# Linear attention, then a gated MLP, on one core: features a step later, outputs held back into the next batch, copies in turns

## The chip, the cores and the metric

The kernel runs on one core of a Trainium2 chip. The metric is the time of the device in microseconds, from the launch's first to its last instruction; the median of several runs counts. The profile is one such execution, whose span (309.5 us) is a little shorter than the time that the runs give.

## The reference

There are 8 batches of 576 tokens. Phase A is attention with 8 heads of 64 channels and random features; phase B is a gated MLP that mixes tokens. Cut to what matters:

```
def phi(x):                                       # x: q or k, 64 channels -> 256 features
    proj = x @ w_phi                              # 128 wide
    proj = proj - max(abs(proj), axis=-1)
    return concat([exp(proj), exp(-proj)])
kv  = einsum('bhsf,bhsd->bhfd', phi(k), v);  z = sum(phi(k), axis=2)
x   = (phi(q) @ kv) / (phi(q) @ z + 1e-6)         # heads side by side: 512 channels

h = relu(x @ w_in);  u, v = h[..., :512], h[..., 512:]
v = (v - mean(v)) / sqrt(var(v) + 1e-6)
v = einsum('ts,bsd->btd', w_spatial, v) + b_spatial
out = (u * v) @ w_out
```

## The kernel before

**Tiles.** Each batch has four main blocks of 128 tokens and a tail of 64. Phase A works in units: a pair unit is two heads of one batch's main tokens, four for each batch; a tail unit is the tails of two batches (a group) for all heads. There are 32 pair units and 4 tail units, numbered in the order in which they run: a group's tail unit, then the four pair units of its even batch, then the four of its odd batch (in the first group one pair unit runs ahead of the tail unit). The program is fully unrolled, and a loop over steps writes out one unit per step, with the stages of earlier units beside it, as a software pipeline.

**One step** (`step`, L589). In step i these pieces are written, in this order, where u is the unit with number i minus a lag (L573):

- `p_features` (L257): `pf`, the projection of q by feature, minus its maximum. Eight small matmuls bring the maximum in from `mT`, two large ones add q's projection. Two PSUM banks. Lag 2.
- `p_keys`, `p_queries` (L266, L269): `pk` and `pq`, the projections by token. Two banks each. Lag 0.
- `e_features` (L272): four exponentials on ScalarE (ACT) turn `pf` into `qf`. Lag 2.
- `r_keys`, `e_keys` (L280, L289): the maximum of `pk` on VectorE (DVE), four exponentials into `kf` on ACT. Lag 0.
- `r_queries` (L294): the maximum of `pq` on DVE, kept in two bf16 parts in `mhl`.
- `a_scale` (L305): `em` on ACT, and v scaled by it into `vs` on GpSimd (POOL).
- `a_num` (L360): the numerators `pn` from `qf` and `kv`, and their division into `x` on DVE. Lag 3.
- `a_max_t` (L332): `mhl` transposed on PE and copied by DVE into `mT` (L335). Lag 1. There are three `mhl` and three `mT`, used in turns.
- `a_kv` (L337): `kv` of two heads on PE, copied out by ACT. Lag 2.
- `a_transpose` (L224) of the next unit, where no DMA has transposed it.
- `a_x_t` (L371): x transposed into `xT`, mostly by DMA. Lag 4. After the last pair unit of a batch, that batch's phase B is pushed into a queue (L631).

From step 8 on (`STRICT`) PE's instructions stay in the order in which they are written; the other engines' order is made by the framework's scheduler.

**Phase B** is a list of tasks for each batch (`b_tasks`, L548): a product for the tail's v, four products for v (`b_v`; ReLU into `vr` on ACT, statistics on DVE), the normalisation on POOL (`b_ln`: a root, L426 to L429, and four times `vn`, L433), four products for u (`b_u`, ReLU on ACT), four products with the spatial weights (`b_s`, each of five matmuls, and the gate on DVE, L493), four output products (`b_o`; `o_mm`, L510, copies the bank into `ob`, and a DMA writes it out), with the tail's tasks between. A task other than `b_s` is four matmuls of 512 columns. Each task takes one PSUM bank, held until the reading engine is through.

**The pace.** `fill` (L577) is called four times in a step. It adds credit, `RATE` = 3.75 us of PE work per step, and starts tasks while the credit covers half of the next one. What is left in the queue after the last step is run at the end (L671 to L673), where the outputs are copied by ACT (`drain`) and elsewhere by DVE (L515).

**PSUM.** All tiles come from one pool of eight banks under one tag (L57).

Of the kernel before, what the change touches and what calls it, by code (L numbers as in the profile page):

```python
# [16 lines left out]
def kernel(  # L17
# [15 lines left out]
    nc = tc.nc  # L33
# [8 lines left out]
    NP = H // 2  # L42
    NB = 4
# [22 lines left out]
    def matmul(**kw):  # L66
        on_pe(nc.tensor.matmul, **kw)

    def transpose(**kw):
        on_pe(nc.tensor.transpose, **kw)  # L70


    def pin(start):
        return lambda *a, **kw: tc.keep_in_program_order(start(*a, **kw))
# [123 lines left out]
    def transpose_spatial(i):  # L198

        pt = psum.tile([P, S], BF16, tag="bank", name="pt")  # L200
        if i < NB:
            sc = POS[i]
            for tp, c in enumerate(POS):
                transpose(out=pt[:, tp * P:(tp + 1) * P], in_=wsp[:, c, bass.ds(sc, P, step=NB)],
                                    identity=ident)
            transpose(out=pt[:, T0:S], in_=wspt[:, bass.ds(sc, P, step=NB)],
                                identity=ident[:TL, :TL])
            nc.vector.tensor_copy(out=w_spT[:, i, :], in_=pt)
            return
        for bl in range(2):  # L210
            lo = bl * TL
            for tp, c in enumerate(POS):
                transpose(out=pt[lo:lo + TL, tp * P:(tp + 1) * P], in_=wspr[:, c, :], identity=ident)
            transpose(out=pt[lo:lo + TL, T0:S], in_=wspt[:, T0:S], identity=ident[:TL, :TL])
            nc.vector.tensor_copy(out=w_spT[lo:lo + TL, NB + bl, :], in_=pt[lo:lo + TL, :])
        for bl, row in ((0, TL), (1, 0)):
            r = slice(row, row + 1)
            pin(nc.scalar.copy)(
                out=w_spT[r, NB + bl, 0:T0].rearrange("o (a b p) -> o a b p", a=2, b=2),
                in_=bsp_row[r, 0:T0].rearrange("o (p b a) -> o a b p", a=2, b=2))  # L220
            pin(nc.scalar.copy)(out=w_spT[r, NB + bl, T0:S], in_=bsp_row[r, T0:S])
# [67 lines left out]
    def e_keys(u, par):  # L289
        for s, sc in ((0, 1.0), (1, -1.0)):  # L290
            nc.scalar.activation(out=u["kf"][:, s, 4 * par:4 * par + 4, :], in_=u["pk"][par], func=AF.Exp,  # L291
                                 bias=0.0, scale=sc)
# [154 lines left out]
    def b_ln(b):  # L447
        d = st[b]
        rstd = root(d["mv"], slice(0, P), NB)
        for j in range(NB):  # L450
            normalize(d["vn"][:, j, :], d["vr"][j], rstd[:, j, :])

    def b_v_tail(g, bls):
        d = gs[g]
        r = slice(bls[0] * TL, (bls[-1] + 1) * TL)
        vr = s2.tile([P, HALF], BF16, tag="vr", name="vr", bufs=5)
        stats = small.tile([P, 6], FP32, tag="stats", name="stats")
        mv = small.tile([P, 1, 2], FP32, tag="mv_t", name="mv_t")
        v_mm(lambda kc: d["xTt"][:, kc, r], vr, r, stats, mv[:, 0, :])
        rstd = root(mv, r, 1)  # L460
        for bl in bls:
            r = slice(bl * TL, (bl + 1) * TL)
            normalize(vnt[g % 2][r, bl, :], vr[r], rstd[r, 0, :])

    def b_u(b, dc):
        d = st[b]
        pu = psum.tile([P, T0], FP32, tag="bank", name="pu")
        for kc in range(KC):
            matmul(out=pu, lhsT=w_in_bf[:, kc, dc * P:(dc + 1) * P], rhs=d["xT"][:, kc, :],
                             start=(kc == 0), stop=(kc == KC - 1))  # L470
        nc.scalar.activation(out=d["uT"][:, dc, :], in_=pu, func=AF.Relu, bias=0.0, scale=1.0)
# [38 lines left out]
    def o_mm(lhs, r):  # L510
        po = psum.tile([P, DM], FP32, tag="bank", name="po")
        for dc in range(KC):
            matmul(out=po[r], lhsT=lhs(dc), rhs=w_out_bf[:, dc, :], start=(dc == 0), stop=(dc == KC - 1))
        ob = s2.tile([P, DM], FP32, tag="ob", name="ob", bufs=5)
        (nc.scalar.copy if drain[0] else nc.vector.tensor_copy)(out=ob[r], in_=po[r])  # L515
        return ob

    def b_o(b, j):
        ob = o_mm(lambda dc: st[b]["uT"][:, dc, j * P:(j + 1) * P], slice(0, P))
        dst = bass.AP(tensor=out.tensor, offset=out.offset + b * S * DM + POS[j] * DM, ap=[[NB * DM, P], [1, DM]])  # L520
        nc.sync.dma_start(out=dst, in_=ob)

    def b_o_tail(g, bls):
        r = slice(bls[0] * TL, (bls[-1] + 1) * TL)
        ob = o_mm(lambda dc: gs[g]["uTt"][:, dc, r], r)
        for bl in bls:
            nc.sync.dma_start(out=out[2 * g + bl, T0:S, :], in_=ob[bl * TL:(bl + 1) * TL, :])


    units = []  # L530
# [8 lines left out]
    NU = len(units)  # L539
# [3 lines left out]
        return units[i] if 0 <= i < NU else None  # L543

    queue = []
    drain = [False]

    def b_tasks(b):  # L548

        g, bl = b // 2, b % 2  # L550
        mm = KC * T0 / 2400.0
        ms = (KC + 1) * T0 / 2400.0
        ts = [(mm, lambda: b_v_tail(g, [bl]))]
        ts += [(mm, lambda j=j: b_v(b, j)) for j in range(NB)]
        ts.append((0.0, lambda: b_ln(b)))
        if b == 0:
            ts += [(0.3, lambda i=i: transpose_spatial(i)) for i in range(NB + 1)]
        ts += [(mm, lambda dc=dc: b_u(b, dc)) for dc in range(KC)]
        tail = g in SPLIT or bl == 1
        bls = [bl] if g in SPLIT else [0, 1]  # L560
        if tail:
            ts.append((mm * len(bls) / 2, lambda: b_u_tail(g, bls)))
        ts += [(ms, lambda dc=dc: b_s(b, dc)) for dc in range(KC)]
        if tail:
            ts.append((ms * len(bls) / 2, lambda: b_s_tail(g, bls)))
        ts += [(mm, lambda j=j: b_o(b, j)) for j in range(NB)]
        if tail:
            ts.insert(len(ts) - 2, (mm, lambda: b_o_tail(g, bls)))
        return ts

    RATE = 3.75
    CAP = 2.5
    LAGS = dict(next=-1, maxima=1, features=2, sums=2, attention=3, out=4)  # L573
    FIRST = dict(next=-1, maxima=1, features=2, sums=2, attention=3, out=3)
    credit = [0.0]

    def fill(share):  # L577
        credit[0] = min(credit[0] + RATE * share, CAP)
        while queue and credit[0] >= queue[0][0] / 2:
            cost, task = queue.pop(0)  # L580
            task()
            credit[0] -= cost

    FT = dict(next=-1, maxima=1, features=2)

    def lag(u, what):
        return (FT if u["i"] == 1 else FIRST if u["pair"] and u["b"] == 0 else LAGS).get(what, 0)

    def step(i):  # L589

        if i == 0:
            a_transpose(units[0])

        def at_work(what):
            return [u for u in units[max(0, i - 5):i + 2] if u["i"] + lag(u, what) == i
                    and (u["pair"] or what not in ("sums", "attention", "out"))]

        def run(what, *fs):
            for u in at_work(what):
                for f in fs:  # L600
                    f(u)

        strict[0] = i >= STRICT
        if strict[0]:
            run("features", p_features)
        run("keys", p_keys)
        run("queries", p_queries)
        if strict[0]:
            run("features", e_features)
        run("keys", r_keys, lambda u: e_keys(u, 0))  # L610
        fill(0.25)
        run("queries", r_queries)
        run("keys", lambda u: e_keys(u, 1), a_scale)
        fill(0.25)
        for u in at_work("attention"):
            a_num(u)
            if u["pj"] == NP - 1:
                finish_batch(u, tail_num)
        fill(0.25)
        if strict[0]:  # L620
            run("maxima", a_max_t)
        run("sums", a_kv)
        run("next", a_transpose)
        if not strict[0]:
            run("features", p_features, e_features)
        fill(0.25)
        for u in at_work("out"):
            a_x_t(u)
            if u["pj"] == NP - 1:
                finish_batch(u, tail_x_t)  # L630
                queue.extend(b_tasks(u["b"]))  # L631
        if not strict[0]:
            run("maxima", a_max_t)
# [21 lines left out]
    for u in units:  # L655
# [4 lines left out]
        if u["pair"] and u["pj"] == 0 and u["b"] > 1:  # L660
# [3 lines left out]
            if u["b"] >= XB:  # L664
                for n, (x, part) in enumerate((("k", 0), ("q", 0), ("k", 1), ("q", 1))):
                    at(u["i"] - XP - 1 + n, cross, u["b"], x, part)
    for i in range(NU + 4):
        step(i)
        for f in io.get(i, []):
            f()  # L670
    drain[0] = True  # L671
    while queue:
        queue.pop(0)[1]()  # L673


# [28 lines left out]
```

## Time and profile before

The median of three runs is 311.28 us (310.86 to 311.39). From the page of the profile:

| | |
|---|---|
| span | 309.5 us, 8463 instructions |
| mean granted clock of TensorE | 0.982 |
| `qf` exponentials (L277, ACT) | 144, 74.4 us busy |
| `kf` exponentials (L291, ACT) | 144, 78.1 us busy |
| maxima of `pk` and `pq` (L286, L298, DVE) | 72 each, 46.4 and 49.9 us busy |
| copies of `ob` (L515) | 32 on DVE, 5 on ACT; full tiles 684 ns on DVE, 587 ns on ACT |
| steps 8 to 35, from `pk` to `pk` | 48.9 us to 259.8 us |

Busy time of an engine is counted with overlapping records joined. A wait is the idle time of an engine ahead of an instruction, put down to what that instruction was waiting for. PE is the stream of matmuls, PEld that of the weight loads, which lie beside it. The windows of the trace give, for a stretch of time, each engine's busy time and number of instructions, the TensorE clock that the throttle granted, and the traffic of the DMA engines. "L62" is the helper through which all matmuls are recorded, so matmuls are told apart by the tiles that they write.

### The profile page before, as it was taken

The page shows a single profiled execution, that of the slowest core. Times are in us where ns is not written, and L with a number is a line of the kernel's source. Part 1 is how long each engine was busy: PE and PEld are TensorE (multiplying, and loading weights), DVE is VectorE, ACT ScalarE, POOL GpSimd, SP SyncE. Part 2 cuts the span into 40 slices and gives each one's busy share as a digit, 9 for nine tenths or more (in the row PEclk, how much of TensorE's full clock was granted, in tenths as well). Part 3 has the DMA queues.
Part 4 walks back from the last instruction along what each step waited for, and adds up shares of the span by engine and source line. Part 5 has one row for each costly group of instructions (what it writes and reads, how often), then busy time and mean ns, then how long its engine had stood idle before and what let it go on. Part 6 is the DMA issues. An engine that isn't in the chain of part 4 may idle for free.

```text
span 309.5 us, 8463 instructions
## 1 busy us (share of the span) xinstructions
PE 255.8 (83%) x3251; PEld 157.4 (51%) x3294; DVE 231.6 (75%) x625; ACT 215.1 (69%) x487; POOL 174.4 (56%) x270
## 2 busy tenths in 40 slices
PE   3279789898997988878887999869797998998983
PEld 1157565666553565444454666435455664553441
DVE  6288997968987799955978799747977796666440
ACT  7558999797597767975487858875587768711603
POOL 8269892885238873497138962497139622620710
PEclk9999999999997999997999999997999999999999
DMA  7979999718652599788942599689912133004005
GB/s 184 233 115 194 205 252 153 168 63 101 153 141 51 84 210 227 147 183 111 155 153 51 154 192 196 161 188 116 207 73 53 17 83 124 4 0 138 0 2 169
DMA packets 82092, 40.35 MB, mean 130 GB/s; under 512 B 50626, under 2 KB 77442, under 8 KB 82052
## 3 DMA queue, kind: packets, MB, share of 16 engines
q1 hardware_dynamic: 54564, 28.33, 40.5%
q0 software_dynamic: 27328, 11.41, 33.5%
q8 instruction: 26, 0.43, 0.6%
q14 instruction: 14, 0.11, 0.1%
q10 hardware_dynamic: 160, 0.07, 0.1%
HBM read 32.85 MB, written 9.44 MB: 137 GB/s over the span
## 4 chain that ended last, share of the span: by engine, by line
PE 28%; DVE 26%; ACT 25%; POOL 8%; issue 7%; DMA 3%; POOLq 0%; DVEq 0%; ACTq 0%; another core or an unknown queue 0%
ACT qf L277 13%; ACT kf L291 9%; PE ps L62 8%; DVE stats L419 7%; PE pf L62 7%; DMA q_tl<-in_q_dram 3%; DVE x L358 3%; POOL vn L433 3%; DVE pq L298 3%; PE pu L62 3%; PE po L62 3%; PE pv L62 3%; DVE mk L286 3%; DVE ob L515 2%; DVE uT L493 2%
## 5 line engine op out<-in xcount | busy, mean ns | idle before, releaser
L277 ACT ACTIVATE qf<-pf 128x512 bf16<-128x512 f32 x144 | 74.4, 606 | 47.6 <-PE pf L62 47.6
L313 POOL TENSOR_TENSOR vs<-v_f,em 128x512 bf16<-128x512 f32 x64 | 65.4, 1041 | 61.9 <-ACT em L308 60.8
L291 ACT ACTIVATE kf<-pk 128x512 bf16<-128x512 f32 x144 | 78.1, 645 | 5.7 <-DVE mk L286 5.7
L286 DVE TENSOR_REDUCE mk<-pk 128x4 f32<-128x512 f32 x72 | 46.4, 686 | 15.1 <-PE pk L62 14.7
L298 DVE TENSOR_REDUCE pq<-pq 128x4 f32<-128x512 f32 x72 | 49.9, 693 | 1.5
L62 PE MATMUL ps<-w_spT,vn 128*128 128x64 bf16 (+1 forms) x244 | 40.6, 288 | 7.8 <-POOL vn L433 6.2
L493 DVE TENSOR_TENSOR uT<-ps,uT 128x512 bf16<-128x512 f32 x32 | 22.0, 687 | 23.8 <-PE ps L62 23.7
L419 DVE BATCH_NORM_STATS2 stats<-vr 128x6 f32<-128x512 bf16 (+1 forms) x40 | 26.9, 680 | 9.2 <-ACT vr L418 9.0
L62 PE MATMUL pu<-xT,w_in_bf 128*128 128x512 bf16 x115 | 32.0, 394 | 2.2 <-ACT kf L291 1.5
L418 ACT ACTIVATE vr<-pv 128x512 bf16<-128x512 f32 (+1 forms) x40 | 22.7, 613 | 14.8 <-PE pv L62 14.3
L62 PE MATMUL po<-w_out_bf,uT 128*128 128x512 bf16 x120 | 30.1, 380 | 1.9 <-ACT kf L291 0.9
L62 PEld LDWEIGHTS <-qf 128*128 128x128 bf16 (+1 forms) x640 | 25.9, 101 | 9.7 <-issue 1.5
L62 PE MATMUL pv<-w_in_bf,xT 128*128 128x512 bf16 x120 | 29.4, 379 | 0.6 <-issue 0.2
L62 PE MATMUL pn<-kv,qf 128*128 128x66 bf16 (+1 forms) x640 | 27.8, 196 | 1.8 <-ACT kf L291 0.8
L62 PE MATMUL pf<-mT,sel 64*128 64x128 bf16 x288 | 16.1, 225 | 14.8 <-DVE mT L335 13.5
L62 PEld LDWEIGHTS <-vn 128*128 128x128 bf16 x256 | 16.6, 99 | 22.1 <-POOL vn L433 9.9
L426 POOL TENSOR_SCALAR var<-mv_t 64x1 f32<-64x1 f32 x8 | 1.9, 239 | 44.3 <-DVE mv_t L420 30.7
L358 DVE TENSOR_TENSOR x<-pn,rc 128x256 bf16<-128x256 f32 x64 | 26.6, 420 | 0.4
L62 PEld LDWEIGHTS <-kf 128*128 128x128 bf16 x640 | 23.3, 99 | 7.0 <-ACT kf L291 2.0
L62 PE MATMUL pv<-vs,kf 128*128 128x66 bf16 x512 | 25.0, 195 | 0.8 <-ACT kf L291 0.8
L433 POOL TENSOR_SCALAR vn<-vr,rs 128x512 bf16<-128x512 bf16 x32 | 24.2, 769 | 0.8
L62 PEld LDWEIGHTS <-w_in_bf 128*128 128x128 bf16 x208 | 15.4, 99 | 14.2 <-issue 3.4
(103 smaller groups left out, 466.5 us busy)
## 6 DMA issues: line engine op xcount, KB each, us to landing
v_f<-in_v_dram SPq DMA_DIRECT2D x8, 1024.0 KB, 7.1
out_dram<-ob SPq DMA_DIRECT2D x32, 256.0 KB, 2.7
k_bf<-in_k_dram POOLq DMA_DIRECT2D x7, 512.0 KB, 6.5
q_bf<-in_q_dram POOLq DMA_DIRECT2D x7, 512.0 KB, 7.7
v_tl<-in_v_dram SPq DMA_DIRECT2D x8, 128.0 KB, 5.1
w_in_bf<-in_moe_w_in_dram POOLq DMA_DIRECT2D x2, 512.0 KB, 8.3
out_dram<-ob SPq DMA_DIRECT2D x8, 128.0 KB, 2.4
k_tl<-in_k_dram POOLq DMA_DIRECT2D x8, 64.0 KB, 7.0
```

The source lines that it names most:

```text
L62: r = f(*a, **kw)
L277: nc.scalar.activation(out=qf[:, s, 4 * par:4 * par + 4, :], in_=u["pf"][par], func=AF.Exp, bias=0.0, scale=sc)
L286: nc.vector.tensor_reduce(out=mk[:, par, :], in_=u["pk"][par], axis=AX.X, op=ALU.max, apply_absolute_value=True)
L291: nc.scalar.activation(out=u["kf"][:, s, 4 * par:4 * par + 4, :], in_=u["pk"][par], func=AF.Exp, bias=0.0, scale=sc)
L298: nc.vector.tensor_reduce(out=mq[:, 4 * par:4 * par + 4], in_=pq[par], axis=AX.X, op=ALU.max, apply_absolute_value=True)
L313: nc.gpsimd.tensor_tensor(out=vs[:, s, :, 0:D], in0=st[u["b"]]["v"][:, pj * H:(pj + 1) * H, :], in1=em[:, s, :].unsqueeze(2).to_broadcast( ...
L358: nc.vector.tensor_tensor(out=x, in0=pn[r, :, 0:D], in1=rc[r].to_broadcast([n, 4, D]), op=ALU.mult)
L418: nc.scalar.activation(out=dst[r], in_=pv[r], func=AF.Relu, bias=0.0, scale=1.0)
L419: nc.vector.bn_stats(out=stats[r], in_=dst[r])
L433: nc.gpsimd.tensor_scalar(out=dst, in0=src, scalar1=rs[:, 0:1], scalar2=rs[:, 1:2], op0=ALU.mult, op1=ALU.add)
L493: nc.vector.tensor_tensor(out=d["uT"][:, dc, :], in0=ps, in1=d["uT"][:, dc, :], op=ALU.mult)
L515: (nc.scalar.copy if drain[0] else nc.vector.tensor_copy)(out=ob[r], in_=po[r])
```

## The change

It does four things, from batch 2 (the second group) on, and the last two everywhere:

- The features of a unit are written one step later (lag 3 in place of 2), and with them the numerators (4 in place of 3) and x (5 in place of 4). The maxima are then a whole step old when `pf` wants them. The loop runs one step longer.
- The output tasks of a batch no longer end its own list. They are kept in `late` and put into the next batch's list, behind the normalisation and ahead of u, so that PE has more work while POOL normalises. The first two batches keep theirs; those of the last batch run at the very end.
- The copies of the outputs go to ACT and DVE in turns, all through.
- The pace is no longer fixed: at the start of each step it is the cost of what is in the queue, divided by the number of steps until the next batch is pushed, at most 4.0.

```diff
-        (nc.scalar.copy if drain[0] else nc.vector.tensor_copy)(out=ob[r], in_=po[r])
+        copies[0] += 1
+        (nc.scalar.copy if copies[0] % 2 else nc.vector.tensor_copy)(out=ob[r], in_=po[r])
...
         if b == 0:
             ts += [(0.3, lambda i=i: transpose_spatial(i)) for i in range(NB + 1)]
+        ts += late[:]
+        late.clear()
         ts += [(mm, lambda dc=dc: b_u(b, dc)) for dc in range(KC)]
...
-        ts += [(mm, lambda j=j: b_o(b, j)) for j in range(NB)]
+        late.extend((mm, lambda j=j: b_o(b, j)) for j in range(NB))
         if tail:
-            ts.insert(len(ts) - 2, (mm, lambda: b_o_tail(g, bls)))
+            late.insert(2, (mm, lambda: b_o_tail(g, bls)))
+        if b < 2:
+            ts += late[:]
+            late.clear()
         return ts
 
-    RATE = 3.75
+    RATE = [0.0]
+    MOST = 4.0
     CAP = 2.5
-    LAGS = dict(next=-1, maxima=1, features=2, sums=2, attention=3, out=4)
+    LAGS = dict(next=-1, maxima=1, features=3, sums=2, attention=4, out=5)
+    SECOND = dict(next=-1, maxima=1, features=2, sums=2, attention=3, out=4)
...
-        credit[0] = min(credit[0] + RATE * share, CAP)
+        credit[0] = min(credit[0] + RATE[0] * share, CAP)
...
-        return (FT if u["i"] == 1 else FIRST if u["pair"] and u["b"] == 0 else LAGS).get(what, 0)
+        return (FT if u["i"] == 1 else LAGS if u["g"] > 0 else FIRST if u["b"] == 0 else SECOND).get(what, 0)
+
+    pushes = [u["i"] + lag(u, "out") for u in units if u["pair"] and u["pj"] == NP - 1]
...
+        left = [p - i + 1 for p in pushes if p >= i]
+        RATE[0] = min(MOST, sum(c for c, _ in queue) / left[0]) if left else MOST
...
-    for i in range(NU + 4):
+    for i in range(NU + 5):
         step(i)
         for f in io.get(i, []):
             f()
-    drain[0] = True
-    while queue:
-        queue.pop(0)[1]()
+    for _, task in queue + late:
+        task()
```

More of the change, by code (lines that the diff above doesn't have):

```diff
@@ L545 @@
     queue = []
-    drain = [False]
+    late = []
+    copies = [0]
     def b_tasks(b):
```

## The prediction

> **What bounds the kernel now.** I read the page's busy row first, then the waits, then the span cut at the starts of steps (the first `pf` of a step on PE), then PE and DVE side by side in two stalls. The busy row:
>
> ```profile
> PE 255.8 (83%) x3251; PEld 157.4 (51%) x3294; DVE 231.6 (75%) x625; ACT 215.1 (69%) x487; POOL 174.4 (56%) x270
> ```
>
> PE looks nearly full, but that is too high: a lone 512-column matmul shows 0.39 us, while eight in a row (pu, at 132.65) take 1.90, so one more costs (1.90 - 0.39)/7 = 0.216 us. I therefore counted PE work from the order of its instructions at columns / 2.4 GHz, half of that for the paired 64-row matmuls (a `pk` group of 8 then starts 0.22 us before the next group, as the trace has it). The stages, in windows of the trace (columns: length, then busy time and count for PE, weight loads, DVE, ACT, POOL; granted clock; DMA):
>
> ```profile
> 48.90:86.60 37.70, 33.76 (x461) 21.76 (x465) 32.84 (x87) 29.97 (x70) 20.27 (x31) 1.00 0.68 127
> 86.60:123.30 36.70, 32.63 (x453) 20.28 (x457) 30.36 (x83) 28.24 (x66) 22.62 (x35) 0.95 1.02 141
> 123.30:191.80 68.50, 58.65 (x775) 36.06 (x787) 54.14 (x144) 50.33 (x118) 42.23 (x66) 0.98 0.92 146
> 191.80:259.80 68.00, 57.74 (x755) 35.47 (x766) 53.91 (x144) 49.74 (x117) 36.96 (x59) 0.97 0.58 119
> ```
>
> I call them S1 (steps 8 to 12), S2 (13 to 17), S3 (18 to 26), S4 (27 to 35); S5 is the rest, 259.8 to 309.5, 49.7 us. By columns PE has 28.9, 27.6, 51.1, 50.7 and 38.2 us of work in them. So in S2 to S4, 173.2 us long, PE works 129.4, ACT is busy 128.3 (74%) and DVE 138.4 (80%): no engine is full, they wait for each other. For what, the table of waits says (total us, times, longest):
>
> ```profile
> ACT qf L277 <- PE pf L62: 47.6, 30, 4.8
> ...
> DVE mk L286 <- PE pk L62: 14.7, 21, 2.1
> ...
> PE pf L62 <- DVE mT L335: 13.5, 12, 1.8
> ...
> PE ps L62 <- POOL vn L433: 6.2, 13, 1.2
> ```
>
> The first two are the echo of the last two: PE stands at `pf`, and `pk`, behind it in PE's order, comes late for DVE and ACT. The DVE timeline before one such stop (start, duration, instruction):
>
> ```profile
> 129.80 0.68 DVE L419 BATCH_NORM_STATS2 stats<-vr 128x6 f32<-128x512 bf16 x1
> 130.40 0.41 DVE L358 TENSOR_TENSOR x<-pn,rc 128x256 bf16<-128x256 f32 x1
> 130.72 0.17 DVE L420 BATCH_NORM_AGGREGATE mv<-stats 128x2 f32<-128x6 f32 x1
> 130.81 0.66 DVE L419 BATCH_NORM_STATS2 stats<-vr 128x6 f32<-128x512 bf16 x1
> 131.39 0.21 DVE L335 COPY mT<-pt 128x128 bf16<-128x128 bf16 x1
> ```
>
> PE gave the transpose at 128.77; DVE copies it at 131.39, behind statistics of phase B, and PE starts `pf` at 131.65 after 1.17 us idle. The other stop, on PE's timeline, and the clock after it (2 us windows, same columns as above):
>
> ```profile
> 138.37 0.39 PE L62 MATMUL ps<-w_spT,vn 128*128 128x512 bf16 x1 [1.22 <-POOL vn L433]
> 139.12 0.39 PE L62 MATMUL ps<-w_spT,vn 128*128 128x512 bf16 x1 [0.37 <-POOL vn L433]
> 139.88 0.39 PE L62 MATMUL ps<-w_spT,vn 128*128 128x512 bf16 x1 [0.36 <-POOL vn L433]
> ```
>
> ```profile
> 138.00:140.00 2.00, 0.90 (x3) 0.29 (x3) 0.00 (x0) 0.29 (x2) 2.00 (x4) 1.00 1.11 290
> 140.00:142.00 2.00, 1.64 (x17) 0.68 (x18) 0.66 (x1) 0.00 (x0) 1.97 (x3) 0.84 0.06 7
> 142.00:144.00 2.00, 1.78 (x20) 1.10 (x18) 1.50 (x4) 1.89 (x4) 2.00 (x4) 0.50 0.87 93
> ```
>
> PE does one matmul per POOL normalisation (0.75 us), DVE and ACT do nothing, and afterwards the clock is halved.
>
> **What the Trainium skill says.** "Perfetto Trace Analysis", Identifying the Most-Contended Engine: matmul busy time does not measure distance from the roofline, occupancy of Vector and Scalar does; the trace agrees (0.216 against 0.39 us), hence my counting. "TensorE: Matmul & The Clock Gate", Part 1: after an idle window of about 3.4 us the PE clock falls to half, and comes back after a busy window. The trace agrees: 0.50 at 98 to 100, 142 to 144 and 210 to 212, each after a stretch with PE mostly idle. "PSUM — Partial Sum Buffer", Engine vs sequencer instructions: Vector and Scalar queues are strict FIFO; so `mT` can't pass the statistics, as seen above.
>
> **The change part by part.**
>
> (1) `pf` of a unit moves from two steps after it to three. Its `mT` is then a whole step old (5.2 us in the shortest step, 122.8 minus 117.55) where DVE was at most 1.83 us late. All twelve waits should go: 13.5, of which 0.5 lies in S1, 0.4 in S5 and 12.6 in S2 to S4. Numerators and x move with it, so their distances to `qf` stay. The buffers that live one step longer (`mT` of 3, transposed q, `qf`) are not rewritten within it: `mT` is rewritten by the unit three later, at step u+4, after its use at u+3. Cost nothing. One step at the start has no `pf`, and one is added at the end; the work is the same.
>
> (2) Held-back outputs. By PE's new order, each batch's list from 3 on runs v, then four or five output products of the batch before, then u, then s (batch 2 has none to take over, but its u is spread over two steps with phase A between). So between v and s lie 8 products or more instead of 4, at 4 x 0.216 = 0.87 us each, while POOL's chain for a batch is 1.9 us of roots and 3.0 of normalising, and was late by 1.22 + 3 x 0.36 = 2.3 us at most. The waits on `vn` go: 4.6 in S2 to S4, 1.5 in the last batch. The half clock goes with them: (0.26 + 0.50 + 0.10) x 2 us = 1.7 for 96 to 102, and the same for 140 to 146 and 208 to 214: 5.1 in all. The first of these is preceded by a `mT` wait (1.82 us), which part 1 takes.
>
> (3) Pace by backlog. Per stage the new order has 24.5, 46.2, 49.6 us of PE work in S2 to S4 (28.5 in S1): 9.1 less, namely 5 output products, 4 spatial products and one step of numerators, which come in S5 instead (47.7 against 38.2). The v products, formerly five in one step (PE work 7.0), are spread over two (5.3), which thins out DVE's statistics.
>
> (4) Copies in turns. Of 37 copies 19 go to ACT, 5 did before: 14 x 0.684 (DVE row) = 9.6 us off DVE, 14 x 0.587 (ACT row) = 8.2 on ACT. In S2 to S4 it is 18 copies, 9 of them on ACT: +5.3, so ACT is busy 128.3 + 5.3 = 133.6. The last copy of all stays on ACT.
>
> Sum for S2 to S4. If every removed wait is gained and nothing else binds: 173.2 - 12.6 - 4.6 - 5.1 - 9.1 = 141.8. But ACT would then be at 133.6 / 141.8 = 94%. Phase A alone, at the start, shows what these in-order queues reach: ACT is busy 26.8 of 30 us between 20 and 50 (89%), 9.7 of 10 between 40 and 50. With B's tasks between I take 88%, a little under the first figure: 133.6 / 0.88 = 151.8, a gain of 21.4. S1: -0.5. S5: +9.5 of work, -1.5 (`vn`), -0.4 (`mT`), with the counting differences of S1 (0.4) taken off: +7.2. So 311.3 - 0.5 - 21.4 + 7.2 = 296.6.
>
> The cost that before does not show is how long PE, no longer held at `pf`, waits for PSUM banks: all tiles share 8, a step takes 13 or 14, and `pf`, `pk`, `pq` hold 6 of them until ACT and DVE are through. From below: today's waits of PE on `kf` and `qf`, 7.8 us over the run (eight rows of 0.8 to 1.5), already paid. From above: all 12.6 us come back as such waits. The 10 us between 141.8 and 151.8 are my allowance for it.
>
> **Rivals.**
> - A, everything is gained: ACT holds 94% as in 40 to 50, S2 to S4 take 141.8. 311.3 - 0.5 - 31.4 + 7.2 = 286.6. For it: in 165.5 to 171.7 PE already did 5.3 us of work in 6.2. Against: it lets ACT wait for nothing over 140 us.
> - B, the bank waits take most of the place of `mT`: S2 to S4 at 84% of ACT, 159.0: 303.8. For it: six banks of eight held early in each step. Against: DVE is relieved by the copies.
> - C, slower: PE is not the limit in S2 to S4, so neither its waits nor the work taken out shorten the steps; only `vn` and clock (9.7) are saved, S5 grows by the full 9.1, and the added step at the end is not filled, 5.4 us (the short step 185.9 to 191.3): 311.3 - 9.7 + 9.1 + 5.4 = 316.1. For it: the shift of work into the drain is certain, the gain is not. Against: the added step stands beside 16 us of B work of batch 6.
>
> **How the numbers follow.** Forecast (290 to 301): 0.52. A (below 290): 0.18. B (301 to 310): 0.20. C: 0.10. The range reaches from A's value to within B: 287 to 309 leaves out some 0.07 below and 0.12 above. Faster: forecast, A and nearly all of B, 0.88; same 0.02; slower 0.10.
>
> **What would show it.** Step 1: no wait of `pf` on `mT` left; waits of `mk` on `pk` far below 14.7. Step 2: `ps` no longer waits for `vn`, clock 1.00 in the middle. Step 3: the last push later relative to the end than now, S5 about 57 us. Step 4: ACT and DVE about even, 223 and 222 us. The prediction is wrong if PE's waits on `kf`, `qf` or on DVE's readers rise by more than 10 us, or if ACT stays below 80% in the middle: at 80% S2 to S4 take 167 and nothing is gained.

## The result, and the profile after

The changed kernel takes 297.64 us (median of four runs, 297.03 to 300.12) against 311.33 us beside it: a ratio of 0.956, 95% interval 0.951 to 0.962. The forecast was 296.6. In a later batch of runs it gave 297.18 us and 0.951 (0.946 to 0.957). Every ratio below compares undisturbed runs with undisturbed runs; of the kernel with the fixed pace, two of four runs, the profiled one among them, were slowed and stand neither in its ratio nor in the sums.

The busy row of the page after:

```profile
PE 258.3 (87%) x3294; PEld 157.7 (53%) x3294; DVE 224.3 (75%) x611; ACT 221.8 (74%) x501; POOL 174.2 (58%) x270
```

Fourteen copies went from DVE to ACT. DVE is busy 7.3 us less and ACT 6.7 us more, somewhat less than the 9.6 and 8.2 that were forecast; the span is shorter. The stages, from the windows (columns as before):

```profile
52.50:93.57 41.07, 37.15 (x458) 22.95 (x455) 31.37 (x84) 30.09 (x69) 21.99 (x33) 0.92 0.60 109
93.57:126.38 32.81, 28.91 (x426) 18.05 (x423) 26.84 (x74) 28.00 (x68) 22.47 (x34) 1.00 1.06 140
126.38:183.67 57.29, 53.53 (x727) 32.21 (x725) 48.90 (x136) 51.59 (x122) 42.01 (x64) 1.00 1.04 170
183.67:241.37 57.70, 55.34 (x762) 33.95 (x759) 49.81 (x136) 51.66 (x121) 36.30 (x57) 1.00 0.73 140
241.37:298.20 56.83, 50.50 (x457) 26.99 (x454) 29.41 (x70) 22.38 (x41) 14.56 (x28) 0.99 0.20 67
```

| us | before | forecast | after | after, second profile |
|---|---|---|---|---|
| start, to step 8 | 48.9 | 48.9 | 52.5 | 51.1 |
| S1 | 37.7 | 37.2 | 41.1 | 39.5 |
| S2 to S4 | 173.2 | 151.8 | 147.8 | 147.8 |
| S5 | 49.7 | 56.9 | 56.8 | 56.8 |

So 25.4 us are gained in S2 to S4 and 7.1 given back in S5, where the held-back work lies. What S1 and the start lost was not foreseen. The start is the same code; what differs is when the tail's keys arrive (PE waits 6.9 us for `k_tl` in this profile, 4.9 in the second, 4.0 before), and that TensorE runs at half clock from 38 to 41 us here, which it did not do in the start before.

The waits after, of the same rows as before:

```profile
ACT qf L277 <- PE pf L62: 19.5, 20, 2.2
...
DVE mk L286 <- PE pk L62: 8.9, 11, 2.0
...
PE ps L62 <- POOL vn L433: 1.0, 3, 0.4
...
PE pf L62 <- DVE mT L335: 0.5, 1, 0.5
```

The one wait on `mT` that is left lies in step 8, before the lag changes. DVE is still late, only nobody stands behind it. DVE's timeline in a step with v products, and `pf` of the same step on PE's:

```profile
137.16 1.28 DVE L419 BATCH_NORM_STATS2 stats<-vr 64x6 f32<-64x512 bf16 x2 [0.86 <-ACT vr L418]
138.36 0.16 DVE L420 BATCH_NORM_AGGREGATE mv_t<-stats 64x2 f32<-64x6 f32 x1
138.44 0.18 DVE L335 COPY mT<-pt 128x128 bf16<-128x128 bf16 x1
```

```profile
137.53 0.40 PE L62 MATMUL pf<-mT,sel 64*128 64x128 bf16 x8
```

The copy at 138.44 is again behind statistics. With the old lag `pf` would have wanted it at 137.53 and stood for a microsecond; now it uses the `mT` of a step ago and starts without idle time. The spatial products and the clock around them (PE's timeline, then 2 us windows):

```profile
150.39 0.39 PE L62 MATMUL ps<-w_spT,vn 128*128 128x512 bf16 x1 [0.36 <-POOL vn L433]
```

```profile
148.00:150.00 2.00, 1.87 (x32) 1.07 (x30) 1.74 (x6) 1.74 (x6) 2.00 (x4) 1.00 1.33 252
150.00:152.00 2.00, 1.64 (x30) 0.96 (x30) 0.89 (x2) 0.36 (x1) 2.00 (x3) 1.00 1.02 80
152.00:154.00 2.00, 2.00 (x10) 0.91 (x11) 2.00 (x4) 2.00 (x5) 0.50 (x2) 1.00 0.86 181
```

One matmul catches up with POOL, the other products find their `vn` ready, and the clock stays at 1.00.

### The profile page after: what moved, and what is told of

It is laid out like the page before. It is cut to its first block, busy times and chain, and to the rows that moved or that the text cites. A ratio compares the mean times of both kernels' runs of the same rounds, so it can differ in the third digit from the quotient of the medians.

```text
span 298.2 us, 8511 instructions
## 1 busy us (share of the span) xinstructions
PE 258.3 (87%) x3294; PEld 157.7 (53%) x3294; DVE 224.3 (75%) x611; ACT 221.8 (74%) x501; POOL 174.2 (58%) x270
## 4 chain that ended last, share of the span: by engine, by line
PE 45%; ACT 31%; DVE 8%; POOL 5%; DMA 4%; issue 4%; ACTq 0%; POOLq 0%; DVEq 0%
ACT qf L277 14%; ACT kf L291 12%; PE ps L62 11%; PE pv L62 9%; PE po L62 9%; PE pu L62 6%; DMA q_tl<-in_q_dram 4%; PE pf L62 4%; PE pt L62 3%; ACT vr L418 3%; PE pn L62 2%; DVE stats L419 2%; POOL vn L433 2%; DVE mk L286 1%; DVE pq L298 1%
## 5 line engine op out<-in xcount | busy, mean ns | idle before, releaser
L277 ACT ACTIVATE qf<-pf 128x512 bf16<-128x512 f32 x144 | 74.6, 616 | 19.6 <-PE pf L62 19.5
L291 ACT ACTIVATE kf<-pk 128x512 bf16<-128x512 f32 x144 | 79.4, 655 | 11.6 <-DVE mk L286 11.6
L62 PE MATMUL ps<-w_spT,vn 128*128 128x512 bf16 (+1 forms) x256 | 39.0, 286 | 1.5 <-POOL vn L433 1.0
L62 PE MATMUL pu<-xT,w_in_bf 128*128 128x512 bf16 x128 | 33.0, 394 | 1.9 <-ACT kf L291 1.8
L62 PE MATMUL po<-w_out_bf,uT 128*128 128x512 bf16 x128 | 31.4, 379 | 1.7 <-ACT kf L291 1.4
L62 PE MATMUL pv<-w_in_bf,xT 128*128 128x512 bf16 x128 | 31.6, 379 | 1.1 <-ACT kf L291 0.3
L62 PE MATMUL pn<-kv,qf 128*128 128x66 bf16 (+1 forms) x640 | 28.9, 196 | 3.2 <-ACT kf L291 2.0
L62 PEld LDWEIGHTS <-qf 128*128 128x128 bf16 (+1 forms) x640 | 25.9, 101 | 10.7 <-issue 3.7
L418 ACT ACTIVATE vr<-pv 128x512 bf16<-128x512 f32 (+1 forms) x40 | 24.0, 622 | 9.5 <-PE pv L62 9.2
L328 POOL TENSOR_TENSOR vst<-v_tl,em 64x512 bf16<-64x512 f32 x16 | 16.4, 1038 | 20.9 <-ACT em L308 20.5
L471 ACT ACTIVATE uT<-pu 128x512 bf16<-128x512 f32 x32 | 20.3, 666 | 10.0 <-PE pu L62 10.0
L62 PEld LDWEIGHTS <-kf 128*128 128x128 bf16 x640 | 24.3, 101 | 6.1 <-issue 2.7
L62 PEld LDWEIGHTS <-w_in_bf 128*128 128x128 bf16 x208 | 16.0, 99 | 15.8 <-issue 3.8
```

Source lines behind the costliest of these rows:

```text
L62: r = f(*a, **kw)
L277: nc.scalar.activation(out=qf[:, s, 4 * par:4 * par + 4, :], in_=u["pf"][par], func=AF.Exp, bias=0.0, scale=sc)
L418: nc.scalar.activation(out=dst[r], in_=pv[r], func=AF.Relu, bias=0.0, scale=1.0)
```

## The experiments

**Each part alone.** The question was whether the time is PE's waits, each part gaining those that it removes, or something else.

The lags alone:

```diff
-    LAGS = dict(next=-1, maxima=1, features=2, sums=2, attention=3, out=4)
+    LAGS = dict(next=-1, maxima=1, features=3, sums=2, attention=4, out=5)
+    SECOND = dict(next=-1, maxima=1, features=2, sums=2, attention=3, out=4)
...
-    for i in range(NU + 4):
+    for i in range(NU + 5):
```

> The kernel before with the lags alone (features, numerators and x one step later from the second group on). Theory W (the time is PE's waits, each part gains the waits that it removes): the wait of pf on mT falls from 13.5 to about 0.5 us, those on vn (6.2) and the half clock after them stay; 311.3 - 12.6 plus some bank waits: 299 to 303. Theory P (what counts is that phase B's products are spread evenly): the statistics still come in one heap, DVE is as late as before, PE stops at PSUM banks in place of mT: 308 to 312. Theory D (DVE's load is the limit): no change, 310 to 312.

Measured: 303.57 us, ratio 0.978 (0.974 to 0.983), just above the 299 to 303 of theory W. The wait of `pf` on `mT` is 0.5 us, that on `vn` grew:

```profile
PE ps L62 <- POOL vn L433: 8.2, 19, 1.1
```

PE comes to the spatial products sooner, POOL does not, so 2 of the 13 us turn into waits on `vn`. PE's waits for readers of PSUM (`kf`, `qf` and DVE's) hardly rise, from 9.3 to 10.6 us; theory P, in which they take the place, falls. But the two waits together are 11.0 us shorter, and 2.2% is only 6.8 us: a wait that is taken away is not gained whole.

The held-back outputs alone:

```diff
+        ts += late[:]
+        late.clear()
...
-        ts += [(mm, lambda j=j: b_o(b, j)) for j in range(NB)]
+        late.extend((mm, lambda j=j: b_o(b, j)) for j in range(NB))
...
```

> The kernel before with the held-back outputs alone. Theory W: the waits on vn (6.2) and two of the three half clocks (3.4) go, the waits on mT (13.5) stay: 301 to 305; of the outputs shifted into the drain nothing is lost where PE was the limit, else up to 3.5 us. Theory P: no gain, since the pace is fixed and the v products still come in one heap; the drain grows by 3.5: 311 to 315. Theory D: 310 to 312.

Measured: 305.85 us, ratio 0.986 (0.981 to 0.992), 0.9 us above the range of theory W. The waits:

```profile
PE pf L62 <- DVE mT L335: 10.9, 9, 2.0
...
PE ps L62 <- POOL vn L433: 2.3, 4, 1.2
```

The wait on `vn` went only in part, and of the three stretches of half clock one went where two were expected: one still follows a stop on `vn` at 139 us, one now follows a wait of 1.99 us on `mT` at 151.

The copies alone:

```diff
-        (nc.scalar.copy if drain[0] else nc.vector.tensor_copy)(out=ob[r], in_=po[r])
+        copies[0] += 1
+        (nc.scalar.copy if copies[0] % 2 else nc.vector.tensor_copy)(out=ob[r], in_=po[r])
```

> The kernel before with the output copies on ACT and DVE in turns alone. Theory W: DVE is 9.6 us less busy, ACT 8.2 more, the waits stay within 2 us: 309 to 312. Theory D: DVE's lateness shrinks, mT comes earlier: 303 to 307. Theory P: 311.

Measured: 311.15 us, ratio 0.998 (0.995 to 1.000). The wait on `mT` is 10.5 us instead of 13.5, and the time hardly changes. DVE's load is not the limit; theory D falls.

The pace by backlog alone:

```diff
-    RATE = 3.75
+    RATE = [0.0]
+    MOST = 4.0
...
+        left = [p - i + 1 for p in pushes if p >= i]
+        RATE[0] = min(MOST, sum(c for c, _ in queue) / left[0]) if left else MOST
```

> The kernel before with the pace by backlog alone. Theory W: the v products lie in two steps, DVE is less late, about half of the 13.5 us on mT goes, the vn waits change little: 304 to 308. Theory P: this is the main part: 298 to 302. Theory D: 310 to 312.

Measured: 325.01 us, ratio 1.050 (1.043 to 1.058). All three theories missed this. The wait on `mT` fell by half, as theory W said, but PE's other one more than trebled:

```profile
PE ps L62 <- POOL vn L433: 21.0, 19, 4.8
PE pf L62 <- DVE mT L335: 5.9, 7, 1.4
```

One such stop on PE's timeline, and POOL's before it:

```profile
108.56 1.36 PE L62 MATMUL ps<-w_spT,vn 128*128 128x512 bf16 x2 [4.24 <-POOL vn L433]
110.81 0.61 PE L62 MATMUL ps<-w_spT,vn 128*128 128x512 bf16 x1 [0.89 <-POOL vn L433]
```

```profile
102.09 0.24 POOL L426 TENSOR_SCALAR var<-mv 128x4 f32<-128x4 f32 x1
102.41 1.04 POOL L313 TENSOR_TENSOR vs<-v_f,em 128x512 bf16<-128x512 f32 x1
103.41 1.05 POOL L427 TENSOR_TENSOR rs<-var,neghalf 128x4 f32<-128x4 f32 x1
104.41 0.22 POOL L315 CAST vs<-em 128x32 bf16<-128x32 f32 x1
104.56 0.80 POOL L74 DMA_DIRECT2D k_tl<-in_k_dram  x1
105.38 0.22 POOL L428 TENSOR_TENSOR var<-mv,rs 128x4 f32<-128x4 f32 x1
105.53 0.70 POOL L74 DMA_DIRECT2D k_tl<-in_k_dram  x1
106.25 0.28 POOL L429 TENSOR_SCALAR rs<-var 128x4 f32<-128x4 f32 x1
106.73 0.96 POOL L74 DMA_DIRECT2D k_bf<-in_k_dram  x1 [0.20 <-issue]
107.74 3.02 POOL L433 TENSOR_SCALAR vn<-vr,rs 128x512 bf16<-128x512 bf16 x4
```

This is batch 2's list. Its last v product now lies in the step after the others, so its statistics come later, and the chain of roots gets in among `vs` of the next unit and three issues of DMAs; from its first instruction to the first `vn` it takes 5.65 us. PE has by then only u to do. The clock, 0.982 before, falls to 0.959.

**Each part left out of the changed kernel.**

> The changed kernel with the old lags (held-back outputs, pace and copies stay). Theory W2 (lag and held-back outputs each remove their waits, and the pace is only harmless because the held-back outputs give POOL time): waits of pf on mT of 5 to 11 us come back, those on vn stay near 1: 302 to 308. Theory S (the four gains add up as they do alone, lag -2.2%, held-back -1.4%, copies -0.2%, pace +5%): 4.4% less than the sum of the rest, that is 320 to 324.

Measured: 308.09 us, ratio 0.990 (0.985 to 0.995): the lag is worth about 3.5% beside the others. The total is at the upper end of theory W2 (302 to 308), its waits are not as it said: 3.8 us on `mT`, less than the 5 to 11 expected, and 6.9 on `vn` instead of about 1. Of these, 5.1 lie in one step:

```profile
111.19 1.36 PE L62 MATMUL ps<-w_spT,vn 128*128 128x512 bf16 x2 [4.24 <-POOL vn L433]
113.44 0.61 PE L62 MATMUL ps<-w_spT,vn 128*128 128x512 bf16 x1 [0.89 <-POOL vn L433]
```

It is the stop of the pace alone, in batch 2's list, which has no outputs to take over. With half clock behind it this step lasts 13.6 us; in the changed kernel it lasts 7.1. So most of the 10 us that the lag is worth here come from this step and not from `mT`. POOL's chain for it, from the root to the first `vn`, again has a `vs` and the three issues of DMAs in it and takes 5.6 us. In the changed kernel batch 2's list runs later, the issues come behind `vn`, and the chain takes 2.1 us (106.89 to 108.98).

> The changed kernel with the outputs at the end of their own list (lag, pace and copies stay). Theory W2: POOL is late again as with the pace alone, vn waits of 15 to 21 us with half clocks behind them: 310 to 320. Theory S: 311.3 x (1 - 0.022 - 0.002 + 0.050) = 319. A theory in which the lag is what makes the pace harmless: 299 to 303.

Measured: 325.53 us, ratio 1.047 (1.042 to 1.052). The lag does not make the pace harmless; `vn` is waited for 20.3 us and the clock is 0.951. The waits are as theory W2 said, the time is above its range.

> The changed kernel with the fixed pace of 3.75 (lag, held-back outputs and copies stay). Theory W2: the waits on mT and vn are gone without the pace too, and the 13.6 us step with the spatial transposes (8.9 before) is not there: 293 to 298, as fast as the changed kernel or faster. Theory P2 (with the held-back outputs in place the even pace brings a part of its own): 300 to 305.

Measured: ratio 0.969 (0.964 to 0.975), that is 302 us, from two runs (301.30 and 302.19 us). So theory P2 holds: with the held-back outputs in place the pace brings 1.3 to 1.8%, although alone it costs 5.0%. By what way it brings them was not traced.

> The changed kernel with the outputs copied by DVE, by ACT only after the last step (lag, held-back outputs and pace stay). Theory W2: nothing waits for DVE by more than a step, ACT is the fuller engine: 296 to 299. A theory in which DVE, now without the stops of PE, is the limit in the middle: 300 to 304.

Measured: 298.01 us, ratio 0.958 (0.953 to 0.963), no difference from the changed kernel that can be told.

**What the held-back outputs do.** Two kernels start from the one without them (325.5 us). In the first, POOL is relieved:

```diff
-            vs = feat.tile([P, 2, H, DA], BF16, tag="vs", name="vs", bufs=4)
-            for s in range(2):
+            vs = feat.tile([P, 1, H, DA], BF16, tag="vs", name="vs", bufs=4)
+            for s in range(1):
...
-                                     rhs=u["vs"][:, s, 4 * hh + c, :], start=(c == 0), stop=False)
+                                     rhs=u["vs"][:, 0, 4 * hh + c, :], start=(c == 0), stop=False)
```

It leaves out the scaling of v for the second sign, so its outputs are not those of the reference; only its time is of use.

> The kernel without held-back outputs (325 us, 20.3 us of waits on vn), and of vs only the product for the first sign is made and used for both: one of two products of 1.04 us each left out in every pair unit, 33 us off POOL in all; PE's order is the same. Theory L (POOL is late with vn because vs and DMA issues stand ahead of it in its queue): waits on vn fall below 10 us and the half clock with them, 305 to 312. Rival (the lateness comes from the statistics on DVE, that is from when the v products are issued): vn waits stay above 15 us, 318 to 325.

Measured: 320.07 us, ratio 1.023 (1.016 to 1.031); POOL is busy 141.6 us instead of 173.9. The wait on `vn` is halved, to 10.4 us, between the two theories, while the time lies in the rival's range. The same stop in the kernel without held-back outputs, and with the lighter POOL:

```profile
145.96 0.39 PE L62 MATMUL ps<-w_spT,vn 128*128 128x512 bf16 x1 [2.82 <-POOL vn L433]
147.47 0.39 PE L62 MATMUL ps<-w_spT,vn 128*128 128x512 bf16 x1 [1.12 <-POOL vn L433]
```

```profile
145.59 0.50 PE L62 MATMUL ps<-w_spT,vn 128*128 128x512 bf16 x1 [1.94 <-POOL vn L433]
146.34 2.11 PE L62 MATMUL ps<-w_spT,vn 128*128 128x512 bf16 x3 [0.25 <-POOL vn L433]
```

The shorter stop, too, is followed by a slow clock: three 512-column matmuls take 2.11 us there and `pn` 2.02 us (1.29 at full clock before), and the mean clock is 0.955. Both steps, from `pk` to `pk`, last 12 us. The traces show what the rest of the lateness is. POOL's chain for this stop, from the root to the first `vn`, without held-back outputs and with the lighter POOL:

```profile
141.12 0.24 POOL L426 TENSOR_SCALAR var<-mv 128x4 f32<-128x4 f32 x1 [1.33 <-DVE mv L420]
...
145.14 3.02 POOL L433 TENSOR_SCALAR vn<-vr,rs 128x512 bf16<-128x512 bf16 x4
```

```profile
141.63 0.24 POOL L426 TENSOR_SCALAR var<-mv 128x4 f32<-128x4 f32 x1 [2.24 <-DVE mv L420]
...
144.76 3.02 POOL L433 TENSOR_SCALAR vn<-vr,rs 128x512 bf16<-128x512 bf16 x4
```

In both POOL stands idle until DVE has the last statistics, so here the rival is right on when the chain starts; the lighter POOL only shortens the chain, from 4.02 to 3.13 us. Both POOL's queue and the late statistics are causes, and a stop cut by half can still be followed by half clock.

In the second, PE gets work that nobody reads, where the held-back outputs stand in the changed kernel:

```diff
+    def idle_work():
+        pi = psum.tile([P, DM], FP32, tag="bank", name="pi")
+        for kc in range(KC):
+            matmul(out=pi, lhsT=w_in_bf[:, kc, 0:P], rhs=w_out_bf[:, kc, :], start=(kc == 0), stop=(kc == KC - 1))
...
+        if b >= 2:
+            ts += [(mm, idle_work) for _ in range(4)]
         ts += [(mm, lambda dc=dc: b_u(b, dc)) for dc in range(KC)]
```

> The kernel without held-back outputs, with four products more that nobody reads, ahead of u in the lists of batches 2 to 7 where the held-back outputs stood: 24 x 0.87 = 20.9 us of PE work added. Theory F (the held-back outputs help because they fill the time in which POOL normalises and keep the clock up): the added work mostly fills waits, vn waits from 20 to below 6 us, clock from 0.951 to above 0.97, time 313 to 322, less than without the added work. Rival (it is the place of the outputs at the end of the list that costs): 340 to 347.

Measured: 313.96 us, ratio 1.005 (1.002 to 1.007). With some 20.9 us more of PE work (an estimate from 24 products at 0.87 us) the kernel is 11.6 us faster than without it. Clock 0.983, and

```profile
PE ps L62 <- POOL vn L433: 0.6, 2, 0.4
```

That is theory F: it is the time between v and s on PE that counts, not the place of the outputs.

**The loss in S1.** In the changed kernel step 9 lasts 13.6 us from `pk` to `pk`; before it lasted 8.8. Step 8 is 2.1 us shorter in return. The new pace puts all six groups of transposes of the spatial weights in step 9. PE's timeline and the windows of the changed kernel:

```profile
65.91 0.58 PE L62 MATMUL pt<-ident,wspr 128*64 128x128 bf16 x4 [2.21 <-DVE w_spT L215]
```

```profile
64.00:66.00 2.00, 0.09 (x2) 0.09 (x2) 1.86 (x8) 1.97 (x6) 1.60 (x3) 0.80 0.51 172
66.00:68.00 2.00, 2.00 (x23) 1.49 (x23) 0.93 (x4) 0.77 (x2) 1.93 (x3) 0.50 0.00 0
68.00:70.00 2.00, 2.00 (x18) 1.17 (x17) 0.77 (x3) 0.58 (x1) 1.83 (x3) 0.50 0.00 0
70.00:72.00 2.00, 2.00 (x15) 0.99 (x13) 0.00 (x0) 0.40 (x2) 1.61 (x4) 0.50 0.00 0
```

PE waits 2.2 us until DVE has copied the transposed weights, and then runs at half clock for more than six. The wait belongs to the new pace, the slow clock not always. In the changed kernel with DVE's copies the same stop was followed by full clock:

```profile
64.67 0.38 PE L62 MATMUL pt<-ident,wspr 128*64 128x128 bf16 x4 [2.21 <-DVE w_spT L215]
```

```profile
51.27:90.57 39.30, 34.24 (x451) 21.44 (x456) 32.51 (x85) 28.57 (x66) 21.98 (x33) 1.00 0.66 115
```

S1 lasts 39.3 us there, 41.1 with the slow clock and 37.7 before. So about half of the 3.4 us lost in S1 is the new order (1.6), the rest came with the slow clock. The order is undone by

```diff
         RATE[0] = min(MOST, sum(c for c, _ in queue) / left[0]) if left else MOST
+        if i <= 12:
+            RATE[0] = 3.75
```

> The changed kernel, but with the pace held at 3.75 up to step 12, so that batch 0's list with the transposes of the spatial weights is spread as in the kernel before (three in step 8, three in step 9) and not all six in step 9. Theory S1 (step 9, 13.6 us in the changed kernel and 8.9 before, is a loss of the new pace): S1 falls from 41.1 to about 37.7, total 293 to 295. Rival (batch 0's work only moves, the later steps get longer by as much): 297 to 298.

Measured: 292.48 us (289.86 to 294.20), ratio 0.936 (0.931 to 0.941), against 297.18 us and 0.951 for the changed kernel in the same batch, for which was expected:

> The changed kernel once more, as the measure for the others on the same chip: 296 to 299, S1 about 41, S2 to S4 about 148.

S1 is 36.3 us at a clock of 1.00, S2 is 1.3 us shorter with the same work on PE (28.8 us busy, 28.9 before this edit), the rest is the same within 1 us:

```profile
50.40:86.69 36.29, 33.74 (x458) 21.36 (x455) 31.29 (x84) 29.18 (x69) 19.97 (x31) 1.00 0.72 131
```

This version beats both kernels. It differs from the changed kernel with the fixed pace only from step 13 on, and there the pace by backlog is worth 0.936 against 0.969.

**The profiles in one sum.** Added up per profile: PE's wait on `mT`, PE's wait on `vn`, and what the slow clock takes at most, (1 - mean clock) x span.

| | on `mT` | on `vn` | clock | sum | span | span - sum |
|---|---|---|---|---|---|---|
| before | 13.5 | 6.2 | 5.6 | 25.3 | 309.5 | 284.2 |
| lag alone | 0.5 | 8.2 | 5.1 | 13.8 | 301.2 | 287.4 |
| held-back alone | 10.9 | 2.3 | 6.4 | 19.6 | 304.1 | 284.5 |
| copies alone | 10.5 | 6.5 | 4.6 | 21.6 | 307.5 | 285.9 |
| pace alone | 5.9 | 21.0 | 13.2 | 40.1 | 321.1 | 281.0 |
| without lag | 3.8 | 6.9 | 10.7 | 21.4 | 306.3 | 284.9 |
| without held-back | 0.5 | 20.3 | 15.8 | 36.6 | 323.2 | 286.6 |
| without copies | 0.5 | 2.2 | 2.4 | 5.1 | 296.2 | 291.1 |
| lighter POOL | 0.5 | 10.4 | 14.3 | 25.2 | 317.9 | 292.7 |
| unread products | 0.5 | 0.6 | 5.3 | 6.4 | 312.7 | 306.3 |
| changed | 0.5 | 1.0 | 5.7 | 7.2 | 298.2 | 291.0 |
| changed, second profile | 0.5 | 1.0 | 4.7 | 6.2 | 295.3 | 289.1 |
| S1 fixed | 0.5 | 0.4 | 2.3 | 3.2 | 289.1 | 285.9 |

Spans that differ by 34 us have remainders between 281.0 and 292.7 (the unread products add 20.9 us of work, which has to be taken off their 306.3). Two waits of PE and its clock are most of the story, though 11.7 us stay open. The clock stands for as much as a wait, but its column is an upper limit: in S1 3.4 us by this sum went with 1.8 us of time. It also differs between runs of one kernel, by 0.981 to 0.992 for the kernel before, that is about 3 us.

## Why the prediction was right, point by point

- **The waits on `mT` (step 1)** went, 13.5 to 0.5, and no bank wait took their place: PE's waits for readers of PSUM are 11.1 us after and 9.3 before. The lag alone brings 2.2% and, beside the others, about 3.5%, much of it through `vn` in batch 2. `mk` still waits 8.9 us for `pk`, not "far below 14.7", and `qf` 19.5 us for `pf`: these waits were an echo of PE's stops only in part.
- **The waits on `vn` and the clock (step 2)** went in S2 to S4: 1.0 us, clock 1.00. The three stretches of half clock, priced at 5.1 us, are gone; what they were worth apart from the waits was not measured. The prediction lets the half clock follow from an idle window of about 3.4 us, but the first of the three came after a stop of 1.82 us.
- **S2 to S4** took 147.8 us for a forecast of 151.8. ACT is busy 28.0 + 51.6 + 51.7 = 131.3 us of them, 88.8% (forecast 133.6 and 88%). That this share was a bound was argued from ACT alone, and does not hold: with the copies back on DVE these stages take 148.7 us with ACT busy 127.4, which is 85.7%. So the 151.8 came near by luck, from a limit that is not there. Of the 6 us between the sum of the removed waits (141.8) and the measured 147.8, 2.9 are waits for readers of PSUM (4.7 to 7.6 us in these stages; the prediction allowed 10) and 1.0 is what is left on `vn`; what the rest is was not traced.
- **S5** took 56.8 us for 56.9.
- **The pace (step 3)** was mis-read. It was taken as a relief for DVE, with nothing said of POOL. It does relieve DVE (`mT` 13.5 to 5.9), but it makes `vn` late by 21.0 us where only u stands between v and s. The forecast held because the change brings the held-back outputs with it, and the lag for batch 2. Step 3 also missed S1, forecast at -0.5 and measured at +3.4 (+1.8 in the second profile): PE's work by columns hardly changes there (28.9 to 28.5), but its order puts six groups of transposes behind each other, which the new order showed.
- **The copies (step 4)**: loads near the forecast (ACT 221.8 for 223, DVE 224.3 for 222), no time of their own.
- **The total** came out at 297.6 for 296.6 in part by luck: S2 to S4 gained 4.0 us more than forecast, and against that S1 lost 3.9 more and the start 3.6 (2.3 and 2.2 in the second profile). Rivals A (286.6) and C (316.1) are excluded by the interval of the ratio, and so is B's value of 303.8.

## What to carry to other kernels

In an in-order pipeline, count what stands on the busiest engine between a producer and the first use of what a slow helper makes of it; changing the pace moves that distance as surely as changing the order does, and an edit that costs 5% alone can gain once the gap is filled. Price a stop of TensorE with the half clock that can follow it, and judge a stage by its work in columns, not by PE's busy share. Where several waits are linked, undo the parts one by one from the finished kernel as well as adding them one by one: here the gains do not add up.

## What was not expected of the hardware

PE need not be quite idle for the clock to fall: in the kernel with the lighter POOL a stop of 1.94 us, one matmul and another stop of 0.25 us were followed by half speed. Nor does a stop of a given length always cost the clock. In the kernel before, the stop of 1.82 us at 95.65 was followed by half speed (0.50 from 98 to 100), an equal one by full speed:

```profile
165.46 0.40 PE L62 MATMUL pf<-mT,sel 64*128 64x128 bf16 x8 [1.83 <-DVE mT L335]
```

```profile
166.00:168.00 2.00, 2.00 (x26) 1.07 (x22) 1.69 (x3) 1.91 (x4) 1.83 (x4) 1.00 0.46 89
168.00:170.00 2.00, 1.61 (x21) 1.02 (x21) 1.86 (x8) 2.00 (x6) 1.73 (x5) 1.00 0.59 108
```

The stop of 2.2 us in step 9 had half clock for 6.8 us behind it in the first profile of the changed kernel, for 3.4 us in the second and for none in the one with DVE's copies. What decides between them is not shown. The length, though, comes in steps. In windows of 1 us over thirteen profiles (all but that of the fixed pace) there are 52 stretches of slow clock. In 40 of them the shortfalls from full clock add up to 1.7 or to 3.4 us, which is 3.4 or 6.8 us at half speed; the other 12 are shorter and lie at the end of a span.

And 20.9 us of matmuls that nobody reads made a kernel 11.6 us faster, with the clock going from 0.951 to 0.983: in the sum above the clock gives 10.5 us and the wait on `vn` 19.7; less the 20.9 that were added, that leaves 9.3 of the 11.6.
